# Decayed keys of the first chunk from a diagonal product on TensorE, in a fused RWKV and GELU-MLP kernel

## The chip, the cores and the metric

One core of one Trainium2 chip runs the whole kernel. The metric is the device time of one execution in microseconds. Three runs of the kernel before took 492.29, 493.2 and 494.58 us; their median is 493.2 us.

## The reference

An attention with a decaying state (RWKV) is followed by an MLP with exact GELU, all in float32. Batch 4, 8 heads, 768 steps, head size 48, model width 384, hidden width 2048.

```
for t in range(S):
    cur = einsum('bhd,bhe->bhde', u * k[t], v[t])
    y[t] = einsum('bhd,bhde->bhe', r[t], state + cur)
    state = w * state + einsum('bhd,bhe->bhde', k[t], v[t])
h = y @ w_in
out = gelu(h) @ w_out
```

## The kernel before

**Chunks and pairs.** Time is cut into 6 chunks of 128 steps, the heads into 4 pairs. The 24 pieces of work are called pairs 0 to 23 here (`gi` in the code, chunk by chunk); pairs 0 to 3 are the first chunk, which the change calls chunk one. Each chunk is handled in two halves of 64 steps.

**One pair.** r and k come transposed (`T`, 448 KB) and are multiplied by powers of w on VectorE (line 402). TensorE makes scores of r against k (`scores`) and, for direct pairs, of r against k times u and w (`own`, from a copy `KB` that ScalarE scales, line 420). VectorE selects the parts of the scores that count into `Am` with two masks (line 527). For the state, k is also needed with time on the partitions and multiplied by decays: it is loaded that way (`N`, with v, 384 KB a pair) and GpSimd multiplies it by a table `WN` of decays (line 409). `WN` is made by VectorE (`state_powers`), turned by TensorE (`flip`, line 330, into bank half `AE[:, 1]`, called O1 in the plan) and copied by ScalarE (line 333). TensorE multiplies decayed k by v (`gains`, line 452); ScalarE (line 508) or VectorE (line 497) turn gains into states. TensorE then makes the outputs from the old state (`old`, line 460) and from `Am` and v (`new`, line 478). ScalarE and VectorE copy them out of the PSUM tile `YU` in two parts, high and low (`keep`, lines 541 and 542). In the first chunk `gaps` (line 491) puts rows of head pair 3 between those of the others.

**Direct pairs.** `DIRECT = 2 * NP` makes pairs 0 to 7 direct. The others load r too (576 KB a pair), and GpSimd multiplies r by k (line 406) and by u (line 424) beside the decay product (line 409); VectorE sums (line 427) and ScalarE writes eight small diagonals into `Am` (line 432).

**MLP.** 16 steps a chunk. A step is nine products of 512 columns in `product1` (line 621, x in two parts against `wh` and `wl`), a GELU on ScalarE (line 650), two splitting operations on VectorE (lines 651 and 652) and nine products in `product2` (line 663). In the first chunk the 16 weight blocks are loaded (768 KB each, line 340) and split into `wh` and `wl`: three ScalarE passes (lines 355, 358, 361), two on VectorE (363, 365), the ScalarE copy to `wh` (367) and the VectorE subtraction to `wl` (369).

**Order.** All work is put down in a list with costs, due times, and names it reads and writes. `Plan.run` (line 86) then fixes the order of each engine: at each moment the engine that can start first takes, of what is ready, the piece that is due first. The hardware queues follow that order. A name that a later piece writes waits for all earlier readers of it. Loads all go through SyncE's queue in the order of `LOADS`; `in_turn` (line 216) lets a load start only when the last but one before it has landed. In chunk one the planner fills the idle time that it expects of TensorE with products of zeros (`heat`, line 286): from the first gains on as many as 0.9 of the expected idle time holds at 110 ns each, 256 columns wide.

## Time and profile before

| what | before |
|---|---|
| profiled execution, us | 493.2 |
| its span, us (first to last instruction) | 491.5 |
| median of 3 runs, us | 493.2 |
| TensorE busy, us (share of the span) | 476.0 (97%) |
| VectorE busy, us | 273.8 (56%) |
| ScalarE busy, us | 174.1 (35%) |
| GpSimd busy, us | 65.7 (13%) |
| mean granted clock of TensorE | 0.997 |

How to read it: PE is TensorE's matmuls, PEld its weight loads, DVE is VectorE, ACT ScalarE, POOL GpSimd, SP SyncE. L452 is line 452. Matmuls are pipelined and overlap, so durations of neighbours add up to more than the time from one start to the next; a timeline's starts are safer than its durations. A wait is put down to the instruction whose signal came last.

### The profile page before, as it was taken

To read this page: it belongs to the slowest core of one execution; us is meant where nothing else is said; L and a number is where in the kernel's file an instruction comes from. 1 tells how busy PE (TensorE), PEld (TensorE's weight loads), DVE (VectorE), ACT (ScalarE), POOL (GpSimd) and SP (SyncE) were. 2 spreads that over 40 slices of the span, in tenths; PEclk is the share of its full clock that TensorE was granted. 3 is DMA by queue.
4 is the path that set the end of the run, shared out by engine and by line. 5 is a ranking of instruction groups with operands and counts; after the bars stand their busy time and mean duration, and the time that the engine had idled before them with its cause. 6 is when DMAs were issued, how large, how long until landed. Compare 5 with 4: busy or idle time off the path is not lost.

```text
span 491.5 us, 11561 instructions
## 1 busy us (share of the span) xinstructions
PE 476.0 (97%) x5052; PEld 385.3 (78%) x5052; DVE 273.8 (56%) x446; ACT 174.1 (35%) x355; POOL 65.7 (13%) x85
## 2 busy tenths in 40 slices
PE   8879999989999999999999999999999999999995
PEld 6768778778888888788878888888888887888884
DVE  7779989995646555626536645554644522322221
ACT  4488988843132133131322331331331311211111
POOL 2210100202202022202022021021120200000000
PEclk9999999999999999999999999999999999999998
DMA  6776586413212313303213403123303000100002
GB/s 179 245 229 232 172 274 233 154 40 123 87 41 59 97 40 96 114 1 98 55 44 97 152 0 97 40 59 97 125 27 97 3 11 12 65 1 0 1 1 69
DMA packets 13192, 43.86 MB, mean 89 GB/s; under 512 B 1809, under 2 KB 2193, under 8 KB 13137
## 3 DMA queue, kind: packets, MB, share of 16 engines
q1 hardware_dynamic: 13136, 43.07, 28.4%
q8 instruction: 41, 0.67, 0.6%
q14 instruction: 15, 0.11, 0.1%
HBM read 36.38 MB, written 4.72 MB: 84 GB/s over the span
## 4 chain that ended last, share of the span: by engine, by line
PE 91%; DVE 6%; ACT 1%; issue 1%; DVEq 0%; ACTq 0%
PE Hp L621 39%; PE O L663 38%; PE A L441 3%; PE Y L460 3%; PE Y L478 2%; PE AE L287 1%; PE Y L452 1%; PE Y L663 1%; DVE wa L365 1%; DVE Am L527 1%; DVE wl L369 1%; DVE wa L363 1%; DVE Tb L402 1%; DVE Sb L497 1%; DVE gl L652 0%
## 5 line engine op out<-in xcount | busy, mean ns | idle before, releaser
L621 PE MATMUL Hp<-xx,wh 128*128 128x512 f32 x576 | 166.5, 397 | 2.3 <-ACT wh L367 2.2
L651 DVE CAST gh<-gf 128x512 fp32r<-128x512 f32 x95 | 44.9, 473 | 171.1 <-ACT gf L650 169.4
L650 ACT ACTIVATE gf<-Hp 128x512 f32<-128x512 f32 x96 | 57.4, 597 | 229.7 <-PE Hp L621 224.8
L621 PEld LDWEIGHTS Hp<-xx,wh 128*128 128x128 f32 x576 | 106.8, 188 | 27.4 <-ACT wh L367 2.6
L621 PE MATMUL Hp<-xx,wl 128*128 128x512 f32 x288 | 83.5, 397 | 2.7 <-DVE wl L369 2.6
L663 PE MATMUL O<-gh,wh 128*128 128x512 f32 (+1 forms) x285 | 82.0, 395 | 0.0
L652 DVE TENSOR_TENSOR gl<-gf,gh 128x512 fp32r<-128x512 f32 x95 | 76.1, 801 | 8.7 <-PE Y L478 0.5
L663 PE MATMUL O<-gl,wh 128*128 128x512 f32 (+1 forms) x285 | 80.6, 390 | 0.3 <-issue 0.3
L663 PE MATMUL O<-gh,wl 128*128 128x512 f32 (+1 forms) x285 | 80.6, 390 | 0.0
L621 PEld LDWEIGHTS Hp<-xx,wl 128*128 128x128 f32 x288 | 53.7, 188 | 17.2 <-DVE wl L369 4.6
L663 PEld LDWEIGHTS O<-gl,wh 128*128 128x128 f32 x285 | 52.5, 188 | 12.3 <-issue 0.7
L663 PEld LDWEIGHTS O<-gh,wh 128*128 128x128 f32 x285 | 52.4, 188 | 12.3
L663 PEld LDWEIGHTS O<-gh,wl 128*128 128x128 f32 x285 | 52.5, 188 | 11.6
L432 ACT ACTIVATE Am<-diag,cs 128x64 f32<-128x64 f32 x128 | 33.9, 338 | 30.3 <-DVE cs L427 30.3
L406 POOL TENSOR_TENSOR Nb<-Nb 128x384 f32<-128x384 f32 x16 | 16.5, 1033 | 135.4 <-DMA Nb<-in_rkv_dram 135.4
L409 POOL TENSOR_TENSOR Nb<-Nb,WN 128x384 f32<-128x384 f32 x20 | 22.7, 1134 | 44.1 <-DMA Nb<-in_rkv_dram 32.6
L402 DVE TENSOR_TENSOR Tb<-Tb,E 112x1024 f32<-112x1024 f32 x20 | 25.1, 1255 | 1.1 <-DMA Tb<-in_rkT_dram 1.0
L497 DVE SCALAR_TENSOR_TENSOR Sb<-Sa,E,Y 48x192 f32<-48x192 f32 x40 | 16.5, 413 | 13.6 <-ACT xx L541 8.3
L424 POOL TENSOR_TENSOR Nb<-Nb,u_sb 128x384 f32<-128x384 f32 x16 | 19.2, 1197 | 0.1
L469 POOL MEMSET turn<- 1x1 f32 x19 | 1.7, 88 | 129.0 <-PE Y L460 129.0
L541 ACT CAST xx<-Y 112x512 fp32r<-112x512 f32 (+1 forms) x18 | 10.6, 587 | 21.6 <-PE Y L452 15.5
L527 DVE COPY_PREDICATED Am<-past,A 128x512 f32<-128x512 uint32 x24 | 17.7, 737 | 0.5
(105 smaller groups left out, 392.8 us busy)
## 6 DMA issues: line engine op xcount, KB each, us to landing
raw<-in_wmlp_dram SPq DMA_DIRECT2D x16, 768.0 KB, 5.4
Nb<-in_rkv_dram SPq DMA_DIRECT2D x16, 576.0 KB, 4.0
Tb<-in_rkT_dram SPq DMA_DIRECT2D x20, 448.0 KB, 4.0
out_dram<-raw SPq DMA_DIRECT2D x5, 768.0 KB, 3.6
xx<-x SPq DMA_DIRECT2D x30, 64.0 KB, 2.3
T<-in_rkT_dram SPq DMA_DIRECT2D x4, 448.0 KB, 4.1
N<-in_rkv_dram SPq DMA_DIRECT2D x4, 384.0 KB, 4.4
Nb<-in_rkv_dram SPq DMA_DIRECT2D x4, 384.0 KB, 3.8
```

What stands on the lines that cost most here:

```text
L402: add("dve", sdve(1024), LATER if g.gi else -10 ** 5, lambda: nc.vector.tensor_tensor(out=flat, in0=flat, in1=E[:, 0, g.p].rearrange("l h ...
L406: add("pool", pool(DM), LATER, lambda: nc.gpsimd.tensor_tensor(out=g.n[:, 0], in0=g.n[:, 0], in1=g.n[:, 1], op=ALU.mult), r=[g.K], w=[g.R])
L409: it = nc.gpsimd.tensor_tensor(out=g.kn, in0=g.kn, in1=WN[:, g.p].rearrange("s j d -> s (j d)").unsqueeze(1).to_broadcast([C, NB, 2 * D]), ...
L424: add("pool", pool(DM), LATER, lambda: nc.gpsimd.tensor_tensor(out=g.n[:, 0], in0=g.n[:, 0], in1=u_sb[:, g.p, :].unsqueeze(1).to_broadcast ...
L432: add("act", sact(HALF) + 60, LATER, lambda x=x, b=b: nc.scalar.activation(out=g.am[:, x, b, :], in_=diag2, func=AF.Copy, scale=g.sums[:, ...
L497: return nc.vector.scalar_tensor_tensor(out=g.s[h + 1][quarter(1 - x)], in0=g.s[h][l], scalar=E[l, 1, g.p, h, MID:MID + 1], in1=gained(g, ...
L527: add("dve", 722, LATER, lambda: nc.vector.copy_predicated(out=g.am, mask=mask.bitcast(U32).unsqueeze(1).unsqueeze(1).to_broadcast([C, 2, ...
L621: nc.tensor.matmul(O[3], lhsT=wt[j][:, 0, k_ * 128:(k_ + 1) * 128], rhs=x[:, a, k_, :], start=start and k_ == ks[0], stop=stop and k_ == k ...
L650: add("act", 600, LATER, lambda: nc.scalar.activation(out=gf, in_=O[3], func=AF.Gelu), r=["H"], w=["gf"])
L651: add("dve", sdve2(512), LATER, lambda: nc.vector.tensor_copy(out=high, in_=gf), r=["gf"], w=[GH])
L652: add("dve", sdve(512), LATER, lambda: nc.vector.tensor_tensor(out=low, in0=gf, in1=high.bitcast(F32), op=ALU.subtract), r=["gf", GH], w=[GL])
L663: nc.tensor.matmul(bank(dst)[:, a:b], lhsT=wt[j][:, 1, d * 128:(d + 1) * 128], rhs=gt[:, a:b], start=(j == 0 and n == 0), stop=(j == NJ - ...
```

## The change

In the first chunk k is no longer loaded with time on the partitions; each load of `N` brings v alone (192 KB). A diagonal matrix `W64` of w to the 64th power is made for each head: GpSimd cuts a small unit matrix from `ident`, ScalarE scales it eight times. For each pair TensorE multiplies the transposed and decayed k with that diagonal, 16 products in two sets with a drain between them, into `AE[:, 1]`, and ScalarE copies the result to where the decayed k stood. The list puts these behind `flip` and its copy, since they write O1 too. The four GpSimd products of the first chunk go. `t2` is loaded before `n0` and `t3` before `n1`. Outputs of the first chunk's pairs alternate between two column ranges of `YU`, each with a name of its own, and a drain stands ahead of `old` for pairs 1 to 3. The state's scalar is read from `P32` and no longer waits for `E1`. Fillers after the first gains have 512 columns and are counted at 234 ns. `DIRECT` is one more, so pair 8 becomes direct.

```
...
 FIRST, STEP, STEP_LAST = 23000, 8400, 3900
 WEIGHT_AHEAD, GROUP_AHEAD, GROUP_DUE = 12500, 28000, 20000
 HEATS, HEAT_NS, HEAT_ROOM = 9, 716, 300
-LOADS = ("t0", "t1", "n0", "t2", "n1", "t3", "w0", "n2", "n3", "w1", "t4", "w2", "n4")
+LOADS = ("t0", "t1", "t2", "n0", "t3", "n1", "w0", "n2", "n3", "w1", "t4", "w2", "n4")
 UNDERWAY, START = 2, 3
 LEEWAY, SHARE = 2000, 0.9
-DIRECT = 2 * NP
+DIRECT = 2 * NP + 1
 
 
 class Plan:
...
         past2 = sb([C, HALF], F32, "past2")
         St = [sb([LP, NP + 1, NB, D], F32, "Sa"), sb([LP, 2, NB, D], F32, "Sb")]
         E = sb([LP, 2, NP, 2, HALF], F32, "E")
-        P32 = sb([LP, 2, 2 * NP], F32, "P32")
+        P32 = sb([LP, 3, 2 * NP], F32, "P32")
         uw = sb([LP, 2 * NP], F32, "uw")
         WN = sb([C, NP, 2, D], F32, "WN")
         T = [sb([LP, 2, NB, C], F32, f"T{i}", pro) for i in range(NP)] + [sb([LP, 2, NB, C], F32, f"Tb{i}") for i in range(2)]
...
         wa = [sb([128, 2 * DM], I32, f"wa{i}") for i in range(3)]
         wb = [sb([128, 2 * DM], I32, f"wb{i}") for i in range(2)]
         ident = sb([C, C], F32, "ident", pro)
+        unit = sb([LP, D], F32, "unit", pro)
+        W64 = sb([LP, 2 * NP, D], F32, "W64", pro)
         ones = sb([C, C], F32, "ones", pro)
         zeros = sb([128, 512], F32R, "zeros", pro)
         warm = sb([128, 1], F32, "warm", pro)
...
 
         def load_kv(gi, at, first=None):
             s = slot(gi)
-            if gi < DIRECT:
-                n = N[s] if gi < NP else N[s][:, 1:]
-                in_turn(lambda: nc.sync.dma_start(n, rkv[gi, :, 1:]), C * 3072, at, [f"Nk{s}", f"Nv{s}"], first)
+            if gi < NP:
+                in_turn(lambda: nc.sync.dma_start(N[s][:, 1], rkv[gi, :, 2]), C * 1536, at, [f"Nv{s}"], first)
+            elif gi < DIRECT:
+                in_turn(lambda: nc.sync.dma_start(N[s][:, 1:], rkv[gi, :, 1:]), C * 3072, at, [f"Nk{s}", f"Nv{s}"], first)
             else:
                 in_turn(lambda: nc.sync.dma_start(N[s], rkv[gi]), C * 4608, at, [f"Nr{s}", f"Nk{s}", f"Nv{s}"], first)
 
...
             for n in range(HEATS):
                 heat((A + [YU[:, 0], YU[:, 1]] + [AE[:, 0], AE[:, 1]])[n % 6])
             plan.filler = lambda: heat(UE[:, 1]), "O0", HEAT_NS, HEAT_ROOM
-            plan.heat = lambda: heat(AE[:, 0, 0:U0], U0), 110, SHARE
+            plan.heat = lambda: heat(AE[:, 0]), 234, SHARE
 
         add("pe", 430 * HEATS, 10, warm_up, r=["zeros"], w=["H", "A0", "A1", "O0", "O1", "Y0", "Y1"])
 
...
             times_one(P32[:, 0].unsqueeze(2), one(E0, MID + 16), one(E0, MID + 16))
             nc.vector.reciprocal(out=P32[:, 1], in_=P32[:, 0])
             times_one(E0[:, :, 0:MID], E0[:, :, MID:HALF], P32[:, 1].unsqueeze(2))
+            nc.vector.tensor_tensor(out=P32[:, 2], in0=P32[:, 0], in1=P32[:, 0], op=ALU.mult)
 
         def state_powers():
             times_one(E1[:, :, 0:MID], E0[:, :, MID:HALF], P32[:, 0].unsqueeze(2))
             times_one(E1[:, :, MID:HALF], E1[:, :, 0:MID], P32[:, 0].unsqueeze(2))
 
-        add("dve", 3000, 5, powers, r=["w_sb"], w=["E0"])
+        def units():
+            nc.gpsimd.memset(unit, 0.0)
+            for x in range(2):
+                l = slice(64 * x, 64 * x + D)
+                nc.gpsimd.tensor_copy(out=unit[l], in_=ident[l, l])
+
+        add("pool", 500, 5, units, r=["ident"], w=["unit"])
+        add("dve", 3070, 5, powers, r=["w_sb"], w=["E0"])
+        for i in range(2 * NP):
+            add("act", 290, LATER, lambda i=i: nc.scalar.activation(
+                out=W64[:, i], in_=unit, func=AF.Copy, scale=P32[:, 2, i:i + 1]), r=["unit", "E0"], w=[f"W64{i}"])
         add("dve", 820, LATER, state_powers, r=["E0"], w=["E1"])
         add("dve", 160, LATER, lambda: nc.vector.tensor_tensor(out=uw, in0=u_lane, in1=one(E0, MID + 1).rearrange(
             "l p i -> l (p i)"), op=ALU.mult), r=["w_sb", "E0"], w=["uw"])
...
                 g.kb, g.KB = KB[i], f"KB{i}"
                 g.sums, g.CS = cs[i], f"cs{i}"
                 g.x, g.X = AA, ["A0", "A1"]
-                g.y, g.Y = YU, ["Y0", "Y1"]
+                g.y, g.Y = (YU[:, :, i * U0:], [f"Y{i}"]) if gi < NP else (YU, ["Y0", "Y1"])
                 g.u, g.U, g.u0 = (UE, ["O2", "O0"], i * U0) if gi < NP else (YU, g.Y, U0)
                 g.s = [St[0][:, gi % SLOTS], St[1][:, i], St[0][:, (gi + NP) % SLOTS]]
                 g.S = [[f"Sa{gi % SLOTS}{x}" for x in range(2)], [f"Sb{i}{x}" for x in range(2)],
...
             if not g.direct:
                 add("pool", pool(DM), LATER, lambda: nc.gpsimd.tensor_tensor(
                     out=g.n[:, 0], in0=g.n[:, 0], in1=g.n[:, 1], op=ALU.mult), r=[g.K], w=[g.R])
+            if g.gi < NP:
+                add("pe", 550, LATER, lambda: decayed(g), r=[g.T, f"W64{2 * g.p}", f"W64{2 * g.p + 1}"], w=["O1"])
+                add("act", 470, LATER, lambda: nc.scalar.copy(
+                    out=g.kn.rearrange("s b (x d) -> s x b d", x=2),
+                    in_=AE[:, 1, 0:2 * NB * D].rearrange("s (x b d) -> s x b d", x=2, b=NB)), r=["O1"], w=[g.K])
+
             def decay():
                 it = nc.gpsimd.tensor_tensor(
                     out=g.kn, in0=g.kn, in1=WN[:, g.p].rearrange("s j d -> s (j d)").unsqueeze(1).to_broadcast(
...
                     after(it, side[g.gi - 1])
 
             beside = g.direct and g.gi >= NP
-            add("pool", pool(DM), LATER, decay, r=["WN"] + ([f"side{g.gi - 1}"] if beside else []), w=[g.K])
+            if g.gi >= NP:
+                add("pool", pool(DM), LATER, decay, r=["WN"] + ([f"side{g.gi - 1}"] if beside else []), w=[g.K])
             if g.direct:
 
                 for h in range(2):
...
                         out=g.am[:, x, b, :], in_=diag2, func=AF.Copy, scale=g.sums[:, 2 * b + x:2 * b + x + 1]),
                         r=["diag20", "diag21", g.CS], w=[g.AM])
 
+        def decayed(g):
+            for i in range(2):
+                if i:
+                    nc.tensor.drain()
+                for b in range(NB):
+                    for x in range(2):
+                        h, at = x ^ i, (x * NB + b) * D
+                        nc.tensor.matmul(AE[times(h), 1, at:at + D], lhsT=g.t[quarter(x), 1, b, times(h)],
+                                         rhs=W64[quarter(x), 2 * g.p + h], start=True, stop=True)
+
         def scores(g, keys=None, col=0):
             for b in range(NB):
                 for h in range(2):
...
                                          rhs=g.vn[times(h), b, heads(x)], start=True, stop=True)
 
         def old(g):
+            if 0 < g.gi < NP:
+                nc.tensor.drain()
             for b in range(NB):
                 for j in range(2):
                     for h in range(1 if g.c == 0 else 0, 2):
...
         def advance(g, h, x):
             l = quarter(x)
             return nc.vector.scalar_tensor_tensor(
-                out=g.s[h + 1][quarter(1 - x)], in0=g.s[h][l], scalar=E[l, 1, g.p, h, MID:MID + 1], in1=gained(g, h, x),
+                out=g.s[h + 1][quarter(1 - x)], in0=g.s[h][l], scalar=P32[l, 2, 2 * g.p + h:2 * g.p + h + 1], in1=gained(g, h, x),
                 op0=ALU.mult, op1=ALU.add)
 
         def gained(g, h, x):
...
                         r=[g.U[0]], w=[g.S[1][1 - x]])
                 else:
                     add("dve", 420, at, lambda x=x: opened(g, advance(g, h, x)) if x == 0 else advance(g, h, x),
-                        r=[g.U[h], g.S[h][x], "E1"], w=[g.S[h + 1][1 - x]] + ([f"side{g.gi}"] if x == 0 else []))
+                        r=[g.U[h], g.S[h][x], "E0"], w=[g.S[h + 1][1 - x]] + ([f"side{g.gi}"] if x == 0 else []))
 
         side = {}
 
...
         def both_states(g):
 
             add("dve", 420, LATER, lambda: opened(g, advance(g, 0, 0)),
-                r=[g.U[0], g.S[0][0], "E1"], w=[g.S[1][1], f"side{g.gi}"])
+                r=[g.U[0], g.S[0][0], "E0"], w=[g.S[1][1], f"side{g.gi}"])
             add("dve", 1260, LATER, lambda: [advance(g, h, x) for h, x in ((0, 1), (1, 1), (1, 0))],
-                r=g.U + g.S[0] + [g.S[1][1], "E1"], w=[g.S[1][0]] + g.S[2])
+                r=g.U + g.S[0] + [g.S[1][1], "E0"], w=[g.S[1][0]] + g.S[2])
 
         def select(g, mask, MASK, col):
             add("dve", 722, LATER, lambda: nc.vector.copy_predicated(
...
             O[0], O[3] = O[3], O[0]
 
         add("do", 0, 0, banks, w=["O0", "O1", "O2", "H"])
-        add("do", 0, 0, swap, w=["late", "ident", "ones", "diag", "past", "zeros", "warm", "spread"] +
+        add("do", 0, 0, swap, w=["late", "ident", "ones", "diag", "past", "zeros", "warm", "spread", "unit"] +
+            [f"W64{i}" for i in range(2 * NP)] +
             [f"{x}{i}" for x in ("T", "Nk", "Nv") for i in range(NP)])
 
         def step_at(m):
```

## Rows read from the trace of the kernel before

**Rows 1.** TensorE's waits, 0 to 62 us: waiter <- releaser, total us, times, longest us.

```profile
PE Hp L621 <- ACT wh L367: 2.2, 1, 2.2
PE Y L478 <- issue: 1.7, 2, 1.0
...
PE Hp L621 <- DVE wl L369: 0.6, 1, 0.6
```

**Rows 2.** TensorE's waits, 62 to 492 us, the same view.

```profile
PE Hp L621 <- DVE wl L369: 2.0, 2, 1.6
```

**Rows 3.** Timeline of TensorE: start us, us, instruction, count, [idle before].

```profile
10.46 0.58 PE L452 MATMUL UE<-N 64*48 64x48 f32 x32 [0.38 <-POOL N L409]
...
17.69 0.65 PE L460 MATMUL Y<-T,Sb 48*48 48x64 f32 x16
19.34 0.66 PE L478 MATMUL Y<-Am,N 64*48 64x64 f32 x32 [1.00 <-issue]
19.93 1.33 PE L287 MATMUL AE<-zeros 128*128 128x256 f32 x9
...
23.91 0.58 PE L452 MATMUL UE<-N 64*48 64x48 f32 x32
...
30.09 0.66 PE L478 MATMUL Y<-Am,N 64*48 64x64 f32 x32
...
35.75 0.96 PE L621 MATMUL Hp<-xx,wh 128*128 128x512 f32 x3 [2.19 <-ACT wh L367]
```

**Rows 4.** Groups of instructions, 0 to 33 us: count | busy us, mean ns.

```profile
L287 PE MATMUL AE<-zeros 128*128 128x256 f32 x43 | 6.9, 296 | 0.0
```

**Rows 5.** Timeline of ScalarE, the same columns.

```profile
8.83 0.48 ACT L333 COPY WN<-AE 128x384 f32<-128x384 f32 x1 [0.96 <-PE AE L330]
...
20.55 0.91 ACT L358 ACTIVATE wb<-raw 128x768 uint32<-128x768 uint32 x1
...
24.60 0.65 ACT L508 COPY Sb<-UE 48x192 f32<-48x192 f32 x2 [2.31 <-issue]
...
27.27 0.59 ACT L541 CAST xx<-Y 128x512 fp32r<-128x512 f32 x1 [1.05 <-PE Y L478]
...
30.82 0.58 ACT L541 CAST xx<-Y 128x512 fp32r<-128x512 f32 x1 [0.75 <-PE Y L478]
...
33.59 0.60 ACT L650 ACTIVATE gf<-Hp 128x512 f32<-128x512 f32 x1 [0.38 <-PE Hp L621]
...
34.88 0.82 ACT L367 CAST wh<-wa 128x768 fp32r<-128x768 f32 x1
```

**Rows 6.** Timeline of VectorE.

```profile
61.19 1.15 DVE L369 TENSOR_TENSOR wl<-wa,wh 128x768 fp32r<-128x768 f32 x1
...
90.52 0.69 DVE L652 TENSOR_TENSOR gl<-gf,gh 128x512 fp32r<-128x512 f32 x1
...
94.13 1.53 DVE L652 TENSOR_TENSOR gl<-gf,gh 128x512 fp32r<-128x512 f32 x1
95.58 1.38 DVE L363 TENSOR_SCALAR wa<-wa 128x768 int32<-128x768 int32 x1
96.88 2.03 DVE L402 TENSOR_TENSOR Tb<-Tb,E 112x1024 f32<-112x1024 f32 x1
98.84 0.95 DVE L369 TENSOR_TENSOR wl<-wa,wh 128x768 fp32r<-128x768 f32 x1
```

**Rows 7.** Timeline of GpSimd.

```profile
94.09 1.02 POOL L406 TENSOR_TENSOR Nb<-Nb 128x384 f32<-128x384 f32 x1 [9.49 <-DMA Nb<-in_rkv_dram]
```

**Rows 8.** DMA issues, 0 to 70 us: count, size, median us to landing.

```profile
raw<-in_wmlp_dram SPq DMA_DIRECT2D x12, 768.0 KB, 5.4
```

**Rows 9.** Timeline of TensorE in an MLP stretch with a direct pair.

```profile
64.62 0.65 PE L441 MATMUL A<-Tb,KB 48*64 48x64 f32 x32
65.09 0.63 PE L478 MATMUL Y<-Am,Nb 64*48 64x64 f32 x32
```

**Rows 10.** VectorE in a window: us, busy us, granted clock, DMA share, GB/s.

```profile
50.00:60.00 10.00, 9.89 (x18) 1.00 0.46 145
```

More of the change, by code (lines that the diff above doesn't have):

```diff
@@ L175, in rwkv_gelu_mlp @@
         E = sb([LP, 2, NP, 2, HALF], F32, "E")
-        P32 = sb([LP, 2, 2 * NP], F32, "P32")
+        P32 = sb([LP, 3, 2 * NP], F32, "P32")
         uw = sb([LP, 2 * NP], F32, "uw")
@@ L192, in rwkv_gelu_mlp @@
         ident = sb([C, C], F32, "ident", pro)
+        unit = sb([LP, D], F32, "unit", pro)
+        W64 = sb([LP, 2 * NP, D], F32, "W64", pro)
         ones = sb([C, C], F32, "ones", pro)
@@ L320, in state_powers, with units @@
             times_one(E1[:, :, MID:HALF], E1[:, :, 0:MID], P32[:, 0].unsqueeze(2))
-        add("dve", 3000, 5, powers, r=["w_sb"], w=["E0"])
+        def units():
+            nc.gpsimd.memset(unit, 0.0)
+            for x in range(2):
+                l = slice(64 * x, 64 * x + D)
+                nc.gpsimd.tensor_copy(out=unit[l], in_=ident[l, l])
+        add("pool", 500, 5, units, r=["ident"], w=["unit"])
+        add("dve", 3070, 5, powers, r=["w_sb"], w=["E0"])
+        for i in range(2 * NP):
+            add("act", 290, LATER, lambda i=i: nc.scalar.activation(
+                out=W64[:, i], in_=unit, func=AF.Copy, scale=P32[:, 2, i:i + 1]), r=["unit", "E0"], w=[f"W64{i}"])
         add("dve", 820, LATER, state_powers, r=["E0"], w=["E1"])
@@ L407, in prepare @@
                     out=g.n[:, 0], in0=g.n[:, 0], in1=g.n[:, 1], op=ALU.mult), r=[g.K], w=[g.R])
+            if g.gi < NP:
+                add("pe", 550, LATER, lambda: decayed(g), r=[g.T, f"W64{2 * g.p}", f"W64{2 * g.p + 1}"], w=["O1"])
+                add("act", 470, LATER, lambda: nc.scalar.copy(
+                    out=g.kn.rearrange("s b (x d) -> s x b d", x=2),
+                    in_=AE[:, 1, 0:2 * NB * D].rearrange("s (x b d) -> s x b d", x=2, b=NB)), r=["O1"], w=[g.K])
             def decay():
@@ L415, in prepare @@
             beside = g.direct and g.gi >= NP
-            add("pool", pool(DM), LATER, decay, r=["WN"] + ([f"side{g.gi - 1}"] if beside else []), w=[g.K])
+            if g.gi >= NP:
+                add("pool", pool(DM), LATER, decay, r=["WN"] + ([f"side{g.gi - 1}"] if beside else []), w=[g.K])
             if g.direct:
@@ L434, in prepare, with decayed @@
                         r=["diag20", "diag21", g.CS], w=[g.AM])
+        def decayed(g):
+            for i in range(2):
+                if i:
+                    nc.tensor.drain()
+                for b in range(NB):
+                    for x in range(2):
+                        h, at = x ^ i, (x * NB + b) * D
+                        nc.tensor.matmul(AE[times(h), 1, at:at + D], lhsT=g.t[quarter(x), 1, b, times(h)],
+                                         rhs=W64[quarter(x), 2 * g.p + h], start=True, stop=True)
         def scores(g, keys=None, col=0):
@@ L455, in old @@
         def old(g):
+            if 0 < g.gi < NP:
+                nc.tensor.drain()
             for b in range(NB):
@@ L797, in rwkv_gelu_mlp @@
         add("do", 0, 0, banks, w=["O0", "O1", "O2", "H"])
-        add("do", 0, 0, swap, w=["late", "ident", "ones", "diag", "past", "zeros", "warm", "spread"] +
+        add("do", 0, 0, swap, w=["late", "ident", "ones", "diag", "past", "zeros", "warm", "spread", "unit"] +
+            [f"W64{i}" for i in range(2 * NP)] +
             [f"{x}{i}" for x in ("T", "Nk", "Nv") for i in range(NP)])
```

24 lines of the change are left out of this document (13 added, 11 removed).

## The prediction

> **What bounds the kernel now.** I read the waits of TensorE first. Before 62 us it waits 2.2 us for `wh` and 0.6 us for `wl`, and stands 1.7 us with no releaser shown ("issue") in front of the products of line 478 [rows 1]; after 62 us it waits twice for `wl`, 2.0 us together, and for nothing else [rows 2]. So whatever moves the MLP's first steps on TensorE moves the end of the kernel by as much, as long as the weights keep up.
>
> The timeline of TensorE over chunk one comes next. The gains of pair 0 start at 10.46, the last output product ends at 30.09 + 0.66 = 30.75, and the second MLP step starts at 35.75 after the 2.2 us wait [rows 3]. The 20.29 us between the first two points hold 43 filling products of 256 columns [rows 4]; nine of them take 1.33 us [rows 3], so 43 take 6.3 us. With 1.7 us of "issue" that leaves 20.29 - 6.3 - 1.7 = 12.3 us for real products. TensorE looks full there, but a third is filling that the planner put where it expected waits: for k and v, GpSimd, and the Y bank.
>
> The timeline of ScalarE shows what the late TensorE costs. From 20.55 (first pass over weight 0) to the end of `wh` for weight 1 at 34.88 + 0.82 = 35.70 are 15.15 us, in which ScalarE waits 2.31, 1.05, 0.75 and 0.38 us for products of TensorE (the first is marked issue, but stands before a copy of gains that TensorE began at 23.91) [rows 3, 5]. So 4.5 us are waits and 10.65 us work. ScalarE's queue, held up by the late gains and outputs of pairs 2 and 3, sets the second MLP step.
>
> Last, the longest wait of the steady part, 1.6 us [rows 2]. It ends with a `wl` that VectorE begins at 98.84, and VectorE lost time just before: 1.53 us for an operation that takes 0.69 elsewhere, then 1.38 and 2.03, while GpSimd ran three products, the first from 94.09 [rows 6, 7].
>
> **The change, part by part.** All four k-with-decay products on GpSimd in chunk one go, and half of each of four loads. Per pair come 16 small products on TensorE with a drain, one copy on ScalarE, and two small scaled copies there.
>
> *Pair 0.* The new product writes the bank half that the transposed table also uses, and is ordered behind its copy: the 0.48 us copy at 8.83 ends at 9.31 and stays on the path [rows 5]. The 16 products are nearest to the 16 of line 460, 0.65 us [rows 3]; with a drain I take 0.75. Bounds: 0.4, if the halves overlap well, and 1.75, with a stand of 1.00 us like that at 19.34. The copy out of PSUM has the table copy's shape: 0.48. That is 9.31 + 0.75 + 0.48 = 10.54, and with 0.4 to 0.5 for handing over and for a scaled pair copy ahead in ScalarE's queue, gains at 11.0 instead of 10.46: +0.5.
>
> *The eight scaled copies* are 112x48. I take 0.25 each, half of the table copy with its 384 elements a partition, 2.0 us in all; bounds are 0 and 0.48 each. They need only the powers table, and ScalarE has no other work between the masks and the first scaled k, so I put them at nothing. If that cover is gone, they cost their 2.0 us. The three tiny GpSimd operations that build the unit matrix run on an idle engine.
>
> *Alternating columns.* Output products of a pair no longer wait until the one before has been copied out of Y. What is late next is the masks, VectorE's work: it keeps five operations per pair.
>
> *Pairs 1 to 3 on TensorE.* Of the 12.3 us, pair 0 has gains and outputs, 0.5 and 1.3, and the other three pairs 3.5 each [rows 3]. To the end of the gains of pair 2 that is 1.8 + 3.5 and, of pair 2, what is not output (1.3 and 0.5): 7.0. With three new products (2.3), the same 1.7 of issue and 0.5 of remaining filling, 11.5 us from 11.0 end at 22.5; before, these gains began at 23.91 and ended about 24.4. The drain added ahead of old products is in none of these numbers: the rows with a drain show 0.1 to 1.00 in front of line 478, and I take the lower end, as these follow at once. The copies of v halve, and with GpSimd gone they stand no longer behind a product. I choose 22.5; from 20.6 (no issue time) to 24.
>
> *ScalarE to weight 1.* Starting its copy of these gains at 22.5, and doing then all of the 10.65 us (weight 0's first two passes, which ran ahead of the copy before, now follow it), ScalarE has `wh` of weight 1 at 33.15 and the second step starts at 33.2 instead of 35.75: **-2.55 us**. Bounds: 0 and -4.2 (from gains at 20.6).
>
> *Loads.* Until weight 1 the cut is 4 x 192 KB, as much as one weight block, which takes 5.4 us from issue to landing [rows 8]. But each load waits for the last but one, and weight 0 stands behind a chain of full-size transposed loads. I take 1 us earlier for weight 1, from 0 to 5.4. ScalarE does not want it before 26, so the loads add nothing.
>
> *Pair 8 is direct.* Two of its three GpSimd products go. VectorE's loss there is (1.53 - 0.69), and about as much on each of the other two: 2.5 us for three. One product stays. The nearest single one cost VectorE about 0.2 (1.15 us at 61.19 against 0.95 at 98.84 for the same operation) [rows 6]; the dearest is 0.84. So 1.65 to 2.3 us come back, at a wait of 1.6. I take **-1.5 us**, from 0 (another order of VectorE's queue) to -1.6.
>
> [...]
>
> *Added for pair 8:* 32 more products on TensorE, 65.09 - 64.62 = **+0.47 us** [rows 9], a mask of 0.75 on VectorE in place of a reduction, and two scaled copies in place of eight small ones on ScalarE. The last two are at nothing: weights are nearly done by then. Without that cover, +0.75.
>
> **Sum:** -2.55 - 1.5 + 0.47 = -3.6 us. The profiled execution took 493.2 us (span 491.5), which is also the median: 489.6.
>
> **Rivals.**
> *A: weights give it back.* Between 50 and 60 us VectorE is busy 9.89 of 10 us [rows 10], so steps 3 to 7 may wait for `wl` by what TensorE gained. For it: `wl` is already waited for in this part (0.6 us) [rows 1], and weights 7 and 8 come through a chain of loads that this change hardly moves. Against it: much of that queue waits for TensorE itself and moves with it. Then of the start only the 1 us counts by which the loads move: 493.2 - 1.0 - 1.5 + 0.47 = 491.2, and without pair 8's gain 492.7.
> *B: ScalarE becomes the bound of chunk one (slower).* Each new product waits until its half bank is copied out, and TensorE's queue stands behind it. A round trip of 0.75 + 0.48, with 0.9 for a scaled pair in front and 0.3 to hand over, is 2.4 us, four times 9.7. If all four stand bare in the place of the 6.3 us of filling, the second step comes 3.4 later: 493.2 + 3.4 - 1.5 + 0.47 = 495.6. It turns slower when these bare waits pass about 7.3 us. Against it: the planner can place each new product well ahead of its gains, since it needs only the transposed k and the scales.
> *C: the clock falls.* [...] The granted clock is 1.00 in the windows I read, such as [rows 10], and after the waits of 1.0 us in chunk one; the pauses left should be no longer. [...]
> *D: more comes out.* Without the issue time the gains of pair 2 end at 20.6: -4.2 - 1.6 + 0.47 = -5.3, 487.9.
>
> **How the numbers follow.** Main line 0.55, A 0.25, B 0.07, C 0.04, D 0.09. A change under 0.5% (2.5 us) cannot be told from none here. Faster by more: nearly all of the main line and D and a small part of A, 0.65. Slower by more (over 495.7): half of B and what nobody listed, 0.07. The rest is 0.28. The range runs from 487.4, a little past D, to 492.6, which takes in A but for its worst and leaves out B and C.
>
> **What would show it.** Right: the first gains near 11.0; far fewer than 43 fillers; gains of pair 2 ending near 22.5; the second MLP step near 33.2; no wait for `wl` near 97 us; no slow VectorE operations in a row before it. The weights' rival shows as waits for `wl` or `wh` between 45 and 75 us that add up to over 2 us; rival B as idle TensorE in front of line 452 or the new line, and the second step after 35.75; C as a granted clock under 1 before 45 us. If the second step starts at 33.2 and the end does not move by some 3 us, the step from start to end is wrong; if it stays at 35, ScalarE's sum is.

## The result and the profile after

The changed kernel takes 499.48 us (median of 11 runs, 497.94 to 501.84), the kernel before, run beside it, 493.65 (11 runs, 492.01 to 498.33): ratio 1.0105, 95% interval [1.0077, 1.0133]. It is slower by about 1%; the forecast was 489.6. The profiled execution took 497.94 us with a span of 496.2, against 493.2 and 491.5 before, so the span grew by 4.7 us.

Timeline of TensorE after, with the columns of [rows 3]; L464 are the new products, L483 the gains, L472 the scores, L511 the outputs, L290 the fillers and L654 the MLP's first products:

```profile
9.06 1.43 PE L464 MATMUL AE<-W,T 48*64 48x48 f32 x32
...
11.08 0.57 PE L483 MATMUL UE<-N 64*48 64x48 f32 x32
11.48 1.22 PE L464 MATMUL AE<-W,T 48*64 48x48 f32 x26
...
14.17 0.58 PE L472 MATMUL A<-T,KB 48*64 48x64 f32 x24 [0.70 <-issue]
...
15.76 1.39 PE L464 MATMUL AE<-W,T 48*64 48x48 f32 x32
...
19.23 0.34 PE L483 MATMUL UE<-N 64*48 64x48 f32 x11 [1.02 <-issue]
...
22.04 0.66 PE L511 MATMUL Y<-Am,N 64*48 64x64 f32 x31
24.28 0.21 PE L511 MATMUL Y<-Am,N 64*48 64x64 f32 x1 [1.58 <-issue]
24.40 0.57 PE L483 MATMUL UE<-N 64*48 64x48 f32 x31
...
24.82 1.35 PE L464 MATMUL AE<-W,T 48*64 48x48 f32 x25
...
30.31 0.89 PE L483 MATMUL UE<-N 64*48 64x48 f32 x32
...
32.52 1.10 PE L511 MATMUL Y<-Am,N 64*48 64x64 f32 x32
...
34.91 1.10 PE L511 MATMUL Y<-Am,N 64*48 64x64 f32 x32
35.94 4.60 PE L290 MATMUL AE<-zeros 128*128 128x512 f32 x12
40.69 0.47 PE L654 MATMUL Hp<-xx,wh 128*128 128x512 f32 x1 [0.15 <-PE AE L290]
...
43.68 0.96 PE L654 MATMUL Hp<-xx,wh 128*128 128x512 f32 x3 [0.69 <-ACT gf L683]
```

The first gains start at 11.08, as forecast (11.0); those of pair 2 start at 24.40 and end near 25.0, where the forecast was 22.5. A set of new products takes 1.4 us and counts 32 records, where 0.75 was taken. TensorE stands three times with no releaser, 3.3 us together against 1.7 [rows 1]. The last output ends at 36.01 instead of 30.75, and the second MLP step starts at 43.68 instead of 35.75 [rows 3]: 7.9 us late.

From 24.4 to 36.01 the same kind of product runs slower: the 32 output products take 1.10 us, 0.66 before. The windows show why (window in us, its length and TensorE's busy time, granted clock, DMA share, GB/s):

```profile
22.00:24.00 2.00, 0.66 (x31) 1.00 0.78 236
24.00:26.00 2.00, 1.64 (x62) 0.93 0.77 294
26.00:28.00 2.00, 2.00 (x72) 0.50 0.68 194
```

TensorE is idle for two thirds of 22 to 24, and from about 25.7 to 39.4 the granted clock is 0.50. Before, it was 1.00 in every window from 8 to 60 us.

Timeline of ScalarE after, with the columns of [rows 5]:

```profile
8.11 0.48 ACT L347 COPY WN<-AE 128x384 f32<-128x384 f32 x1
...
24.53 0.58 ACT L574 CAST xx<-Y 128x512 fp32r<-128x512 f32 x1 [4.23 <-PE Y L511]
25.14 0.65 ACT L541 COPY Sb<-UE 48x192 f32<-48x192 f32 x2
26.53 0.48 ACT L424 COPY N<-AE 128x384 f32<-128x384 f32 x1 [0.75 <-PE AE L464]
...
31.31 0.65 ACT L541 COPY Sb<-UE 48x192 f32<-48x192 f32 x2 [2.72 <-issue]
...
36.08 1.07 ACT L574 CAST xx<-Y 128x512 fp32r<-128x512 f32 x2 [3.14 <-PE Y L511]
37.03 0.84 ACT L381 CAST wh<-wa 128x768 fp32r<-128x768 f32 x1
...
42.07 0.84 ACT L381 CAST wh<-wa 128x768 fp32r<-128x768 f32 x1 [0.25 <-DVE wa L379]
```

The copy of pair 2's gains starts at 25.14, and `wh` of weight 1 ends at 42.07 + 0.84 = 42.91. In these 17.8 us ScalarE waits 0.75, 2.72, 3.14 and 0.25 us, 6.9 together, where the forecast had none; its work is 10.9 us, near the forecast's 10.65. At 36.08 ScalarE copies the outputs of pairs 2 and 3 in one go. Those of pair 2 were finished at 32.52 + 1.10 = 33.62; the copy still waited for pair 3's, which end at 36.01, and `wh` of weight 0, queued behind it, waited as well.

TensorE's waits after 62 us, the view of [rows 2]:

```profile
PE Y L483 <- issue: 1.0, 1, 1.0
PE Hp L654 <- DVE wl L383: 0.4, 1, 0.4
PE O L696 <- issue: 0.4, 1, 0.4
```

The 1.6 us wait for `wl` is gone, as forecast for pair 8, but TensorE now stands 1.0 us with no releaser at 94.08, in the same stretch. The second step is 7.9 us late and the end only 4.7, so 3.2 us came back. Part is in the MLP's products from 120 to 480 us, first of the kernel before and then of the changed one (count | busy us, mean ns | idle before):

```profile
L621 PE MATMUL Hp<-xx,wh 128*128 128x512 f32 x468 | 134.7, 396 | 0.0
...
L663 PE MATMUL O<-gh,wh 128*128 128x512 f32 x220 | 65.4, 402 | 0.0
```

```profile
L654 PE MATMUL Hp<-xx,wh 128*128 128x512 f32 x470 | 134.0, 393 | 0.0
...
L696 PE MATMUL O<-gh,wh 128*128 128x512 f32 x224 | 66.0, 400 | 0.0
```

The clock is 1.00 there in both, and the products are the same; each is 2 to 3 ns shorter. Nothing in the prediction speaks of that.

### The profile page after: what moved, and what is told of

Its sections match the earlier page's. It is cut to its first block, busy times and chain, and to the rows that moved or that the text cites. A ratio compares the mean times of both kernels' runs of the same rounds, so it can differ in the third digit from the quotient of the medians.

```text
span 496.2 us, 11839 instructions
## 1 busy us (share of the span) xinstructions
PE 479.9 (97%) x5184; PEld 391.2 (79%) x5184; DVE 273.3 (55%) x447; ACT 176.4 (36%) x361; POOL 66.4 (13%) x82
## 4 chain that ended last, share of the span: by engine, by line
PE 91%; DVE 5%; issue 2%; DMA 1%; ACT 0%; SPq 0%; DVEq 0%
PE Hp L654 38%; PE O L696 38%; PE A L472 3%; PE Y L493 3%; PE Y L511 3%; PE Y L483 1%; PE Y L696 1%; DVE wl L383 1%; PE AE L290 1%; PE AE L464 1%; DMA T<-in_rkT_dram 1%; DVE Am L560 1%; DVE wa L379 1%; PE Y L524 1%; PE UE L483 1%
## 5 line engine op out<-in xcount | busy, mean ns | idle before, releaser
L654 PE MATMUL Hp<-xx,wh 128*128 128x512 f32 x576 | 164.9, 394 | 0.8 <-ACT gf L683 0.7
L684 DVE CAST gh<-gf 128x512 fp32r<-128x512 f32 x95 | 47.2, 497 | 167.9 <-ACT gf L683 166.4
L654 PEld LDWEIGHTS Hp<-xx,wh 128*128 128x128 f32 x576 | 106.8, 188 | 24.9 <-ACT gf L683 1.1
L654 PE MATMUL Hp<-xx,wl 128*128 128x512 f32 x288 | 82.9, 395 | 1.9 <-DVE wl L383 1.9
L685 DVE TENSOR_TENSOR gl<-gf,gh 128x512 fp32r<-128x512 f32 x95 | 73.2, 771 | 8.4
L654 PEld LDWEIGHTS Hp<-xx,wl 128*128 128x128 f32 x288 | 53.7, 188 | 15.5 <-DVE wl L383 3.6
L453 ACT ACTIVATE Am<-diag,cs 128x64 f32<-128x64 f32 x120 | 31.8, 338 | 29.2 <-DVE cs L448 29.2
L429 POOL TENSOR_TENSOR Nb<-Nb,WN 128x384 f32<-128x384 f32 x20 | 29.3, 1466 | 76.7 <-DVE Sa L530 29.0
L530 DVE SCALAR_TENSOR_TENSOR Sb<-Sa,P,Y 48x192 f32<-48x192 f32 x40 | 16.5, 413 | 15.0 <-ACT xx L574 9.9
L445 POOL TENSOR_TENSOR Nb<-Nb,u_sb 128x384 f32<-128x384 f32 x15 | 17.6, 1177 | 0.1
```

Source lines behind the costliest of these rows:

```text
L429: it = nc.gpsimd.tensor_tensor(out=g.kn, in0=g.kn, in1=WN[:, g.p].rearrange("s j d -> s (j d)").unsqueeze(1).to_broadcast([C, NB, 2 * D]), ...
L445: add("pool", pool(DM), LATER, lambda: nc.gpsimd.tensor_tensor(out=g.n[:, 0], in0=g.n[:, 0], in1=u_sb[:, g.p, :].unsqueeze(1).to_broadcast ...
L453: add("act", sact(HALF) + 60, LATER, lambda x=x, b=b: nc.scalar.activation(out=g.am[:, x, b, :], in_=diag2, func=AF.Copy, scale=g.sums[:, ...
L530: return nc.vector.scalar_tensor_tensor(out=g.s[h + 1][quarter(1 - x)], in0=g.s[h][l], scalar=P32[l, 2, 2 * g.p + h:2 * g.p + h + 1], in1= ...
L654: nc.tensor.matmul(O[3], lhsT=wt[j][:, 0, k_ * 128:(k_ + 1) * 128], rhs=x[:, a, k_, :], start=start and k_ == ks[0], stop=stop and k_ == k ...
L684: add("dve", sdve2(512), LATER, lambda: nc.vector.tensor_copy(out=high, in_=gf), r=["gf"], w=[GH])
```

## The experiments

The questions: what makes chunk one late (longer products, the stands, the halved clock, fillers, the copy that waits for the wrong pair), and where the 3 us come back. Ahead of the single runs, what they gave; "ratio" is to the kernel before, run beside each.

| kernel | last output ends, us | second MLP step, us | ratio [95%] |
|---|---|---|---|
| before | 30.75 | 35.75 | 1 |
| changed | 36.01 | 43.68 | 1.0105 [1.0077, 1.0133] |
| e1 changed, clock held by fillers | 36.89 | 44.34 | 1.0157 [1.0123, 1.0191] |
| e2 before, pair 8 direct | 32.58 | 37.58 | 1.0012 [0.9989, 1.0035] |
| e3 before, alternate columns | 29.85 | 35.44 | 1.0021 [0.9985, 1.0057] |
| e4 changed, block-diagonal products | 34.56 | 42.01 | 1.0107 [1.0067, 1.0148] |
| e5 changed, no new products | 32.24 | 40.39 | 1.0031 [1.0008, 1.0054] |
| e6 before, wide fillers | 31.37 | 35.87 | 1.0004 [0.9972, 1.0036] |
| e7 changed, one load under way | 41.81 | 50.59 | one run, 541.77 us |
| e8 changed, columns as before | 37.20 | 41.60 | 1.0091 [1.0067, 1.0116] |
| e9 before, tiles moved by 32 bytes | 30.37 | 35.34 | 0.9943 [0.9922, 0.9964] |
| e10 before, tiles moved by 64 bytes | 30.07 | 35.06 | 0.9932 [0.9900, 0.9964] |
| e11 changed, three things mended | 35.22 | 39.65 | 1.0014 [0.9986, 1.0042] |
| e12 as e11, no fillers in the gaps | 32.32 | 37.16 | 0.9953 [0.9929, 0.9978] |

### e1: the clock held up by fillers

```diff
         def decayed(g):
+            for _ in range((0, 0, 4, 2)[g.gi]):
+                heat(AE[:, 0])
...
         def gaps(g):
+            for _ in range((0, 6, 3, 3)[g.gi]):
+                heat(AE[:, 0])
```

> The changed kernel with 18 more filling products of 512 columns in chunk one: 4 ahead of the new product of pair 2, 2 ahead of that of pair 3, and 6, 3 and 3 ahead of the gap rows of pairs 1, 2 and 3. At 0.23 us each they add 4.1 us of TensorE work. Theory 'clock' (the change loses because TensorE ran at the half granted clock from about 25.7 to 38.6 us): the granted clock stays at 1.00, the second MLP step starts near 37 us instead of 43.68, and the kernel is 4 to 6 us faster than the changed one, within 1 us of the kernel before. Theory 'supply' (TensorE stands for its next instructions about every 128 products as the profile counts them, some 5 us apart, and the clock only follows): the stands of 1.02 and 1.58 us shrink by about the fillers put ahead of them, but the second step still comes no earlier than about 37. Rival 'ScalarE chain': the clock is no matter, the second step stays at 43 or later.

The second step did not come near the 37 us of the clock theory. The clock now falls only between 28 and 34 us (0.80, 0.50 and 0.85 in windows of 2 us), behind one stand that is longer than any in the changed kernel:

```profile
28.82 0.45 PE L474 MATMUL A<-T,KB 48*64 48x64 f32 x13 [2.07 <-issue]
...
36.23 0.66 PE L513 MATMUL Y<-Am,N 64*48 64x64 f32 x32
36.83 3.03 PE L290 MATMUL AE<-zeros 128*128 128x512 f32 x12
```

Outputs are back at 0.66 us, yet the last one ends at 36.89, later than without the fillers. The 18 extra fillers cost at least what the clock gave back, and the kernel is slower than the changed one (1.0157 against 1.0105). A clock bought with fillers is no gain here.

### e2, e3 and e6: three parts of the change alone, in the kernel before

```diff
-DIRECT = 2 * NP
+DIRECT = 2 * NP + 1
```

> The kernel before with pair 8 direct and nothing else changed. Theory 'port' (the 1.6 us wait for wl near 99.8 us comes from three GpSimd products slowing VectorE): that wait falls under 0.3 us, 0.47 us of products come in, the time falls by 0.8 to 1.4 us (ratio 0.9970 to 0.9985). Rival 'moved': the one product left still holds VectorE up, or another wait takes the place, ratio 1.000 to 1.002.

```diff
-                g.y, g.Y = YU, ["Y0", "Y1"]
+                g.y, g.Y = (YU[:, :, i * U0:], [f"Y{i}"]) if gi < NP else (YU, ["Y0", "Y1"])
...
         def old(g):
+            if 0 < g.gi < NP:
+                nc.tensor.drain()
```

> The kernel before with outputs of chunk one in alternating columns of Y and the drain ahead of old products, and nothing else changed. Theory 'order': pairs 1 to 3 no longer wait for the copies out of Y, the planner puts fewer fillers, and the second MLP step comes 0 to 1.5 us earlier, ratio 0.997 to 1.000. Theory 'supply': fewer fillers bring nothing, as the stands grow by as much, ratio 1.000 to 1.002. Rival 'clock': with fewer fillers the granted clock falls below 1.00 in chunk one also here, ratio over 1.004.

```diff
-            plan.heat = lambda: heat(AE[:, 0, 0:U0], U0), 110, SHARE
+            plan.heat = lambda: heat(AE[:, 0]), 234, SHARE
```

> The kernel before with fillers of 512 columns, counted at 234 ns, after the first gains, and nothing else changed: about 18 in place of 43. Theory 'supply': 25 products fewer are worth 25 x 0.039 = 1.0 us, the second MLP step starts 0.5 to 1.2 us earlier, ratio 0.997 to 0.9995. Theory 'clock': fewer fillers let the granted clock fall in chunk one, ratio 1.002 to 1.008. Rival 'no matter': 0.9995 to 1.002.

None of the three makes a difference that can be measured. In e2 TensorE's waits after 62 us fall from 2.0 us for `wl` to 0.4:

```profile
PE Hp L621 <- DVE wl L369: 0.4, 1, 0.4
PE O L663 <- issue: 0.3, 1, 0.3
```

So the wait that the step "pair 8 is direct" counts on is gone. But the 1.6 us are not a fixed price: of the kernels that keep the three GpSimd products, e9 waits for `wl` 1.6 us at the longest after 62 us, e6 and e3 0.8. The interval reaches down to 0.9989, 0.5 us, so the net 1.0 us forecast (1.5 - 0.47) doesn't reach the end. In the profiled execution chunk one lost 1.8 us in exchange: the stands are 3.3 us instead of 1.7, and the second step starts at 37.58. Why stands grow in a stretch that this edit doesn't touch stays open. In e6 the clock was 0.50 to 0.91 from 18 to 24 us at hardly any loss (last output at 31.37), since the kernel before has room there.

### e4, e5 and e8: three parts undone in the changed kernel

```diff
...
-            for i in range(2):
-                if i:
-                    nc.tensor.drain()
-                for b in range(NB):
-                    for x in range(2):
...
+            for b in range(NB):
+                for h in range(2):
+                    nc.tensor.matmul(AE[times(h), 1, 2 * D * b:2 * D * b + 2 * D], lhsT=g.t[:, 1, b, times(h)],
+                                     rhs=W64[:, 2 * g.p + h], start=True, stop=True)
```

> The changed kernel with the diagonal product of both heads in one product of 112 rows by 64 against a block diagonal of 96 columns: half as many products, no drain, the same result. Theory 'supply': 64 products of the profile's count go from the stream (half of one 128), the new product of a pair takes 0.4 to 0.6 us instead of 1.35, the first gains come 0.7 us earlier, and gains of pair 2 end 2 to 3 us earlier than 24.8. Theory 'clock': if the granted clock still falls (about as few fillers stand there as in the changed kernel), the kernel stays slower than before by over 1 us; if it holds, it is at 490 to 492.

Eight wide products in place of 16 take 0.88 us for 16 records, and the last output ends 1.45 us sooner:

```profile
21.86 0.54 PE L478 MATMUL UE<-N 64*48 64x48 f32 x32
22.33 0.88 PE L459 MATMUL AE<-W,T 112*64 112x96 f32 x16
25.83 0.64 PE L467 MATMUL A<-T 48*64 48x64 f32 x29 [2.62 <-issue]
...
33.46 1.10 PE L506 MATMUL Y<-Am,N 64*48 64x64 f32 x32
```

The gains of pair 2 end at 22.40, where the prediction had them, but the first gains are no earlier (11.23). A stand of 2.62 us and half the clock (0.50 from 28 to 36) remain, and a further stand of 2.54 at 57.9. The time is that of the changed kernel: half the products alone are worth nothing that can be measured at the end.

```diff
-                if i:
-                    nc.tensor.drain()
...
-                        nc.tensor.matmul(AE[times(h), 1, at:at + D], lhsT=g.t[quarter(x), 1, b, times(h)],
-                                         rhs=W64[quarter(x), 2 * g.p + h], start=True, stop=True)
+                        pass
```

> The changed kernel without the new diagonal products on TensorE and their drain: the copies on ScalarE stay and read what the bank half holds, so k of chunk one is wrong and the products' time is left out. It has the profile's 128 products fewer, one full stretch between two stands, which came every 126 to 127 products in all six traces so far. Theory 'supply' (in chunk one TensorE gets its instructions no faster than about 40 ns a product, so each product added costs that, whatever it computes): the last output product of chunk one ends near 11 + 526 x 0.039 = 31.5 us instead of 36.0, the second MLP step starts near 39 instead of 43.68, ratio 0.998 to 1.003. Theory 'clock': the granted clock falls here too, as fillers are as few, and the ratio stays over 1.006. Rival 'ScalarE copies' (the four copies and the eight scalings hold ScalarE's queue): the last output still ends after 34 us.

Without any new product the last output still ends 1.5 us later than before, and the second step 4.6 later. So the products, with their drain, are the larger part of the loss, 3.7 us (1.0105 to 1.0031, give or take 1.8 by the two intervals), but not all of it. The last output and the second step lie some 1 us past what the supply theory asked, and the ratio is far below the 1.006 of the clock theory. What is left in e5 is a hole of 3.66 us on TensorE, put down to VectorE, half the clock behind it (0.50 from 24 to 36), and the copy that waits for the wrong pair:

```profile
24.54 2.08 PE L521 MATMUL Y<-x,spread 112*128 112x256 f32 x8 [3.66 <-DVE wa L377]
...
31.14 1.10 PE L508 MATMUL Y<-Am,N 64*48 64x64 f32 x32
```

e8 gives the outputs their columns of before:

```diff
-                g.y, g.Y = (YU[:, :, i * U0:], [f"Y{i}"]) if gi < NP else (YU, ["Y0", "Y1"])
+                g.y, g.Y = YU, ["Y0", "Y1"]
...
         def old(g):
-            if 0 < g.gi < NP:
-                nc.tensor.drain()
```

> The changed kernel with the outputs of chunk one all in the same columns of Y again and without the drain ahead of old products. Theory 'false wait' (ScalarE's wait of 3.14 us at 36.08 us is for the last output product of pair 3, though it copies pair 2, because the alternate columns are ordered as one): ScalarE copies pair 2 before the outputs of pair 3 are made, wh of weight 0 is done 1 us or more before the last output product ends plus 1.9 us, and the second MLP step comes 1 to 2 us earlier than in the changed kernel, ratio 1.006 to 1.009. Rival 'supply': the products are as many, the ratio stays at 1.009 to 1.012.

ScalarE copies pair 2's outputs at 31.78, right behind them, and the second step starts 2.1 us sooner although the last output ends 1.2 later. The distance between the two parts the kernels: 7.7, 7.5, 7.5 and 8.2 us in the changed kernel, e1, e4 and e5, which have alternate columns and the new order of work; 4.4 in e8, 4.4 and 4.8 in e11 and e12, and 5.0 before. At the end the gain cannot be told from none: 1.0091 against 1.0105. Nor are the 3 us between the two groups of distances the copy's alone. In the four kernels with the late copy 12 fillers stand behind the last output and hold up the first MLP step; in the changed kernel it ends at 42.99, as late as `wh` of weight 1 (42.91), so the second step would hardly come sooner with the copy alone put right. No run parts the two. In e8 nine fillers stand ahead of pair 3's outputs:

```profile
31.50 0.87 PE L483 MATMUL UE<-N 64*48 64x48 f32 x32
32.29 2.76 PE L290 MATMUL AE<-zeros 128*128 128x512 f32 x9
...
41.60 0.97 PE L652 MATMUL Hp<-xx,wh 128*128 128x512 f32 x3 [2.11 <-ACT gf L681]
```

### e7: one load under way at a time

```diff
-UNDERWAY, START = 2, 3
+UNDERWAY, START = 1, 3
```

> The changed kernel with every load waiting for the one before it, so one is under way at a time where two were. [...]

The loads come far too late and the kernel takes 541.77 us. Only the stands are of interest: in the first 62 us they fall from 3.3 us to 0.2.

```profile
PE Hp L654 <- ACT wh L381: 5.4, 1, 5.4
...
PE Y L493 <- issue: 0.2, 1, 0.2
```

So they go with the load traffic; the evidence is weak, as TensorE is held up by other things here and asks for less in a time.

### e9 and e10: nothing but a shift of addresses

P32 gets an unused row more (e9), or two (e10), as it has one more in the changed kernel. No instruction of the source differs from before; every tile placed behind P32, the MLP's inputs among them, lies 32 or 64 bytes further on.

```diff
-        P32 = sb([LP, 2, 2 * NP], F32, "P32")
+        P32 = sb([LP, 3, 2 * NP], F32, "P32")
```

> The kernel before with one edit that no instruction uses: P32 gets a third row, so every tile placed behind it lies 32 bytes further on. In the stretch from 120 to 480 us the mean of one 512-column MLP product is 396 and 395 ns (first products) and 389 to 390 ns (second products by the low halves) before, 393 and 387 to 388 after, in every variant of the changed kernel as well, and as before in every variant of the kernel before. Theory P (placement): the 32 bytes carry this. Then the products go to 393 and 388 here, some 1,400 of them by 2 to 3 ns make 3.5 us, and the time is 490 us, 0.993 of before. Rival Q (something else of the change, such as the order of loads or the decay tile): the products stay at 396 and 390 and the time is 493.5, 1.000. Chunk one is the same either way: second MLP step at 35.7.

> The same with two rows, so the tiles lie 64 bytes further on. If where a tile begins within a piece of 64 bytes decides, the products stay at 396 and 390 and the time at 1.000 of before. If any shift does it (theory P without a rule on alignment), they go to 393 and 388 and the time to 0.993. If the products of the 32-byte kernel don't move, these don't either.

From 120 to 480 us in e9:

```profile
L621 PE MATMUL Hp<-xx,wh 128*128 128x512 f32 x471 | 134.2, 393 | 0.0
...
L663 PE MATMUL O<-gh,wh 128*128 128x512 f32 x222 | 65.7, 400 | 0.0
```

(The 389 to 390 ns of e9's expectation are means over products of 512 and of 256 columns; those of 512 alone go from 396 to 394.) The products are those of the changed kernel, 393 and 400 ns, and both kernels are faster than before by 2.8 and 3.4 us (0.0057 and 0.0068 of 493.7). Placement is shown as the cause, and a rule that only the place within 64 bytes counts falls, since the shift by 64 does as well. Which of the moved tiles matters was not tried. It also gives the change's own price: 1.0105 / 0.9943 = 1.0163 or 8.0 us (give or take 1.7 by the two intervals), about the 7.9 by which the second step is late. e9 and e10 beat both kernels.

### e11 and e12: the change mended

e11 joins e4's products, e8's columns and the fillers of before. (Its expectation gives these 64 columns; they have 256, [rows 4].) e12 takes out, besides, the fillers of the planned gaps:

```diff
-            plan.heat = lambda: heat(AE[:, 0, 0:U0], U0), 110, SHARE
```

> The changed kernel with three things mended at once: the new products as 16 wide ones by a block-diagonal matrix, the outputs in their columns of before (no false wait, no drain), the fillers those of before (64 columns, counted at 110 ns). Theory S (supply: TensorE gets only so many products a time while the weights are loaded, and each new product takes what an old one would have had): 32 fewer records than in the changed kernel, so the last output ends near 34, a stand of 1.7 to 2.7 us comes after some 250 to 370 records, and the second MLP step starts at 39 to 40.5, still 3.5 us behind before; the time is 1.003 to 1.008 of before. Rival K (the halved clock and the false wait make the loss): with both gone the second step comes at 35 to 37 and the time is 0.993 to 0.998, the MLP products at 393 and 388 included.

> The mended kernel without the fillers that the order of work puts into chunk one's planned gaps (the nine ahead of it and the two wide ones stay). In the mended kernel 21 of its 28 fillers run in one stretch of 3.89 us at half clock, at 29.51, while ScalarE waits 2.60 us for the outputs behind them (copy at 35.27, wh of weight 1 at 38.26). Theory F (the planned gaps aren't there on the chip, since TensorE is late, and the fillers stand in the path): the last output ends at 31 to 31.7 instead of 35.22, ScalarE's copy comes near 31.5, wh of weight 1 near 34.7, the second MLP step at 35.5 to 36.5 instead of 39.65, and the time is 0.993 to 0.997 of before, the faster MLP products included. Rival K (the fillers are what keeps the clock up): the clock falls earlier or for longer than 24 to 32, the outputs stretch by as much as the fillers took, the last output ends at 34 to 36 and the time stays at 1.000 to 1.004. Rival S (supply alone): the stand that came after 375 products comes after as many, so some 1 us is gained for the 28 products less, and the last output ends near 34.

e11 came out at 1.0014, below the range of the supply theory, though its interval reaches into it and its second step, 39.65, lies in it; that the clock and the late copy alone make the loss falls, with the step at least 2.6 us behind what that asked. The stands, 0.77 and 1.39 us, were smaller than expected. The timeline showed what was left:

```profile
28.72 0.87 PE L478 MATMUL UE<-N 64*48 64x48 f32 x32
29.51 3.89 PE L290 MATMUL AE<-zeros 128*128 128x256 f32 x21
33.24 0.63 PE L517 MATMUL Y<-x,spread 112*128 112x256 f32 x4
```

Twenty-one fillers run in one piece between the gains and outputs of pair 3. e12 takes them away:

```profile
18.75 0.71 PE L466 MATMUL A<-T,KB 48*64 48x64 f32 x24 [2.04 <-issue]
...
21.73 1.10 PE L503 MATMUL Y<-Am,N 64*48 64x64 f32 x32
...
31.66 0.66 PE L503 MATMUL Y<-Am,N 64*48 64x64 f32 x32
...
37.16 0.96 PE L646 MATMUL Hp<-xx,wh 128*128 128x512 f32 x3 [1.73 <-ACT gf L675]
```

The clock did fall, as rival K said, to 0.50 from about 19 to 26 us behind the stand of 2.04, but it was then back at 1.00, and the last output ends at 32.32 instead of 35.22. The fillers in the planned gaps cost 2.9 us of chunk one and, from 1.0014 to 0.9953, about 3.0 us at the end (give or take 1.8). That puts the time within what the filler theory expected, though the last output and the second step are 0.6 and 0.7 later than its ranges. e12 beats the kernel before, but not e9: without its faster products (0.9953 / 0.9943 = 1.0010) the mended change is worth nothing that can be measured.

## Why the prediction was wrong

**What bounds the kernel: right.** A delay of the second MLP step does move the end by about as much: 7.9 us, and 8.0 at the end once placement is set apart; for e11 the same two are 3.9 and 3.5. The weights did not take it back (rival A): TensorE waits for `wl` 1.5 us before 62 us, where it was 0.6, and 0.4 us after, where it was 2.0.

**Pair 0: right in the sum, by luck.** Gains at 11.08 against 11.0, though the products took 1.43 us and not 0.75: the table's copy ended at 8.11 + 0.48 = 8.59, where the sum kept 9.31.

**Pairs 1 to 3 on TensorE: failed, by 2.5 us.** The gains of pair 2 end near 25.0 and not at 22.5. The terms:
- *The products.* I set 16 products of the source beside a row that counts 16, line 460 at 0.65 us. But the profile counts two records for such a product: the 16 in the source show as 32, and cost 1.4 us. Ahead of pair 2's gains this hardly shows, by luck again: three sets were charged there, 2.3 us, and only two ran, some 2.5 us. The third stands behind these gains, at 24.82, and so do pair 3's scores.
- *The issue time.* I kept 1.7 us as a constant; it was 3.3, and that is most of the 2.5. Stands come with the records: before, after 138 and 265 records from the first gains; after, after 104, 230 and 357; in e4 after 121, 248 and 374. The distance is 126 or 127 each time, so work added moves the stands and can bring a further one. It need not: the kernel before passes its third place, near 392 records, without a stand, and e2, with the same work there, stands 0.71 us.
- *The filling.* I took all but 0.5 us of its 6.3 as room, and as far as pair 2's gains that was right (0.73 us at 17.07). But the order of work is written from planned times, so it keeps fillers for gaps that TensorE, late on the chip, no longer has. Of the 14 left in the changed kernel 12 stand behind the last output, 4.60 us, where they delay the first MLP step; with the columns undone they stand in the path, and e12 shows their price there, about 3 us.

(The bound of 20.6 without issue time is 20.8 by its own sum, 22.5 - 1.7.)

**ScalarE to weight 1: the step that failed most.** `wh` of weight 1 ends at 42.91 and not at 33.15, 9.8 us late. The late gains make 2.6 of it (copy at 25.14 instead of 22.5) and the work 0.3. The other 6.9 are waits, which I put at nothing because pair 2's gains would come earlier. But ScalarE's queue also takes the gains and outputs of pair 3, and my sum for TensorE ended at pair 2. Behind it came the third set of products, pair 3's scores and eight products for the rows in the gaps (`spread`), in good part at half the clock: pair 3's gains start at 30.31, where they started at 27.02 before, and its outputs end at 36.01. In e4 the gains of pair 2 did end as forecast, at 22.40, and the second step was still at 42.01.

**Alternating columns: no gain seen.** I let outputs lose a wait and the masks come next. In their new order ScalarE's copy of pair 2 waits for pair 3's outputs, and 12 fillers come to stand behind the last output; undoing the columns brings the second step 2.1 us sooner (e8), with no difference at the end that can be measured. In the kernel before the same columns make none either (e3). Why the copy waits for products in other columns is only argued: both are parts of one tile, and pair 3's products stand ahead of the copy in the order written.

**Rival C, a falling clock, named the event, with 0.04, and mispriced it.** I argued that pauses would be no longer than the 1.0 us in which the clock had held. The new one is 1.58 us, and the clock fell some 1.4 us behind it, to 0.50; in e6 it fell to 0.50 behind a stand of 1.00, but in e2 it held at 1.00 behind one of 1.83. I charged 4.2 us (493.8 in all), for the nine MLP products of two steps at half the clock. That was my estimate, and no run shows the sum: in the changed kernel it was chunk one's own products that stretched, by 2.7 us in those rows that can be compared (two sets each of outputs and old products by 0.44, the gains by 0.32, eight spread products by 0.6). The MLP's products slowed in e2, e3, e6 and e9, which need no new product for it: there the granted clock fell behind the 2.2 us wait for `wh` (means of 0.50 to 0.66 in windows of 2 us), and in e9 the second step takes 6.2 us and not 4.7; in the kernel before and in e10 it stayed at 1.00 behind a wait as long. In the changed kernel 0.50 came behind the stretch from 22 to 24 us, in which TensorE was busy for 0.66 us. That the clock alone made the loss, however, e1 and e12 speak against.

**Rival B, the slower one, was not it.** TensorE does not stand for the copies out of the half bank; its idle time from the first gains to the last output shows no releaser.

**Pair 8: right in its place, not fixed in size, absent at the end.** With pair 8 direct the longest wait for `wl` after 62 us is 0.4 us in the changed kernel and e2, 0.7 in e5, 0.8 in e1 and e12, and e4 has none; but of the kernels without it e3 and e6 wait no longer than 0.8 either, and e2 alone gains nothing that can be measured. (After 62 us the kernel before also stands 0.3 us with no releaser, which I left out.) The loads' step, at nothing, holds as far as seen.

What stays open: how the loss in chunk one divides exactly between products, stands, clock, fillers and the late copy, since each edit moved the others; and the sum of single gains (1.45 in e4, 2.1 in e8, 2.5 in e12) is not one of independent terms.

## What to carry to other kernels

Ask what a row counts before dividing by it: an instruction of the source can be two records (here 16 products were 32), and a price per record applied per instruction halves a cost. Fillers in an order fixed beforehand are free only while the engine keeps that order's times; once it is late they are work like any other (2.9 us of chunk one, e12), so an edit that adds work must be followed by a look at where each filler has come to lie. Carry a sum on to the last piece of work that the path passes: here it ended at pair 2, and the waits for pair 3 made most of the miss. And before crediting a change, see whether instructions that it doesn't touch changed their length: here an added row of a small table moved the steady part by 3 us, and hid a third of the loss.
